# Another order for the same instructions: a written-out plan of a fused SSM-convolution and gated-MLP backward pass

## The chip, the cores and the metric

One core of a Trainium2 chip. The metric is the device time of one execution in microseconds (us), as a median of runs; a profile of one execution shows where it goes. The engines are TensorE (PE, matmuls; PEld is its weight load), VectorE (DVE), ScalarE (ACT), GpSimd (POOL) and SyncE (SP, which here issues every DMA).

## The reference, cut to what matters

The kernel computes a forward pass and all its gradients for a given `grad_out`, with S = 2048 tokens, D = 512, F = 1376, in bf16. The input x is normalised once and goes through two layers:

```python
xn = layernorm(x)
# layer A: shift convolution (4 taps), product with v, long convolution by FFT over 2S
k_shift = sum(k_pad[:, t:t + S, :] * shift_k[:, ks - 1 - t] for t in range(4))
kv = k_shift * v
y = irfft(rfft(kv) * rfft(ssm_k))[:S] + kv * ssm_D
# layer B: bilinear gated MLP
h = (xn @ w_gate) * (xn @ w_up)
out = x + xn * y + h @ w_down
```

The outputs are `out` and the gradients of x, k, v, of the shift taps, the long convolution's kernel and ssm_D, and of the three weight matrices (w_gate, w_up: D x F; w_down: F x D).

## The kernel before, in words

The kernel is written as a set of small steps, each on one engine, and an order for all of them. Helper objects stand in for the engines: a call such as `nc.vector.tensor_tensor` only records an `Op` (class `Eng`, line L173, which is why nearly every row of the profile carries L173). Consecutive matmuls into the same PSUM tile are joined to one PE step of up to 2200 columns. There are 2285 steps: 1009 of PE (3190 matmuls and transposes in all), 654 of DVE, 361 of ACT, 258 of SP (one DMA each) and 3 of POOL.

At the end `emit(PLAN)` decodes a string: a permutation of the 2285 steps, and then one bank number for each of 398 PSUM tiles (8 banks of 512 fp32 columns; a two-bank tile takes a neighbouring pair). It issues the steps in that order under a manual schedule. So each engine's queue holds its own steps in the order of the plan, and semaphores follow from what the steps read and write. A PSUM bank's next owner waits until the last reader of the owner before is through.

SP's DMAs go out in plan order from one queue, with eight semaphores taken in turn: a DMA waits for its own data and also for the landing of the eighth DMA before it, and all that stand behind it wait with it.

The steps by stage, with the names that matter below (n, r and j are indices that the code uses):

- Loads and layer norm: `xload`, `gtload` (columns of transposed grad_out, `goT`), the first MLP weights in two transfers (L364 and L368), `gload` (grad_out rows, `go`), `w_load(j)`. `ln` normalises x rows; `tr_rows` (L409 to L416) transposes them, on PE for rows under 8, by DMA transpose otherwise.
- `mlp_rows(j, r)` (L429 to L440): for six stages j of F, the gradient towards the hidden layer (`pd`, from goT, which needs only goT and weights) and the two gates (`pg`, from the normalised, transposed x). ACT, in some stages DVE, evicts; DVE forms the products. `hd_store` writes products to a DRAM buffer HD.
- `dw_gen(j)` (L589 to L606): weight gradients, groups of 16 matmuls accumulating over 16 row tiles. They lie among the other steps.
- `a_gen`: shift convolution and the first step of the Fourier transform for three signals (stored to AX). `s_gen` (`s_B`, `s_pw`, `s_Bi`): the middle step, products in the frequency domain, and the way back (stored to CX).
- `turn_gen` (L620 to L627): transposes of hidden products of stages 4 and 5, partly by DMA, partly on PE.
- The last part, for n = 0 to 7 (two of the 16 row tiles each): `c_load(n)` reads 1.5 MB of CX, `last_dft(n)` (24 matmuls) forms three signals, `c_dkv`, `c_y`, `c_o5` use them, `c_dsk` multiplies by k (`k_load`) and sums on PE with ones (8 matmuls per row tile). `hd_load(n)` (L645) reads HD by a DMA transpose into buffer n % 2, which must wait for the last matmul of n - 2 that reads it. `y_o(n, rr)` (11 matmuls, plus one with the identity for n = 7) and `y_x(n, rr)` (22) multiply its blocks by the three weight matrices for the output and for x's gradient; y_x has a chain of DVE steps behind it (L815 to L821, with ACT at L820) that ends the layer norm's gradient. `dk_pair` (seven DVE steps and a store) forms k's gradient. For n = 7 y_o(rr=1) runs in two halves of 256 columns.

Of the kernel before, what the change touches and what calls it, by code (L numbers as in the profile page):

```python
# [25 lines left out]
SB = [0, None, 1, 2, 3, 4]  # L26
# [12 lines left out]
def kernel(  # L39
# [895 lines left out]
    for n in range(NCH):  # L935
# [148 lines left out]
```

## Time and profile before

| what | value |
|---|---|
| time, median of 3 runs | 427.82 us (427.53 to 428.08) |
| the profiled execution | 426.92 us, of which the span of the core's instructions is 425.1 us |
| TensorE clock granted | 1.00 of full speed over the span |
| DMA | 127.27 MB, 299 GB/s on average, one queue at 94.4% of 16 engines' span |
| matmuls | first at 1.06 us, last ends at 420.10 us |
| largest group of PSUM evictions | ACT, 314 of them, 781 ns on average |

The span is the time from the first to the last instruction of the profiled execution; 1.8 us of the execution's time lie around it. A row of waits gives the engine and line, whom it waited for, the total in us, how often, and the longest. The chain of waits follows the work that ended last back to the start, each row with start, duration and what it was. Since all recorded steps have one line, tiles tell the steps apart: `PP` is PSUM, `big` the SBUF, `AX`, `CX`, `HD`, `KS` are DRAM buffers and `in_..._dram`, `out_dram` the inputs and outputs.

### The profile page before, as it was taken

The page shows a single profiled execution, that of the slowest core. Times are in us where ns is not written, and L with a number is a line of the kernel's source. Part 1 is how long each engine was busy: PE and PEld are TensorE (multiplying, and loading weights), DVE is VectorE, ACT ScalarE, POOL GpSimd, SP SyncE. Part 2 cuts the span into 40 slices and gives each one's busy share as a digit, 9 for nine tenths or more (in the row PEclk, how much of TensorE's full clock was granted, in tenths as well). Part 3 has the DMA queues.
Part 4 walks back from the last instruction along what each step waited for, and adds up shares of the span by engine and source line. Part 5 has one row for each costly group of instructions (what it writes and reads, how often), then busy time and mean ns, then how long its engine had stood idle before and what let it go on. Part 6 is the DMA issues. An engine that isn't in the chain of part 4 may idle for free.

```text
span 425.1 us, 8146 instructions
## 1 busy us (share of the span) xinstructions
PE 414.8 (98%) x3190; PEld 198.9 (47%) x3190; DVE 350.7 (82%) x684; ACT 257.8 (61%) x364; POOL 3.5 (1%) x9
## 2 busy tenths in 40 slices
PE   7999999999999999999999999999999999999995
PEld 4745555854554333544444334444444444444343
DVE  5999977998649989899999980325858898999996
ACT  4855988598644999888999953363414230422323
POOL 1000000000000000000000000000000000000000
PEclk9999999999999999999999999999999999999999
DMA  8999899999788879969889899999999999999953
GB/s 277 399 180 395 295 305 395 344 363 360 298 297 304 320 250 338 310 202 341 305 286 349 291 313 314 250 392 309 188 296 305 308 258 333 309 303 290 278 174 147
DMA packets 104222, 127.27 MB, mean 299 GB/s; under 512 B 63860, under 2 KB 73977, under 8 KB 103160
## 3 DMA queue, kind: packets, MB, share of 16 engines
q1 hardware_dynamic: 104184, 126.75, 94.4%
q8 instruction: 25, 0.41, 0.4%
q14 instruction: 13, 0.11, 0.1%
HBM read 57.10 MB, written 54.04 MB: 261 GB/s over the span
## 4 chain that ended last, share of the span: by engine, by line
PE 70%; DVE 14%; DMA 11%; issue 2%; ACT 2%; SPq 1%; ACTq 0%
PE PP L173 70%; DVE big L173 14%; DMA out_dram<-big 4%; DMA big<-CX 2%; DMA big<-in_k_dram 2%; ACT big L173 2%; SPq L173 1%; DMA big<-in_w_dram 1%; DMA big<-in_go_dram 1%; DMA big<-in_x_dram 1%; ACTq L1080 0%
## 5 line engine op out<-in xcount | busy, mean ns | idle before, releaser
L173 PE MATMUL PP<-big 128*128 128x512 bf16 (+7 forms) x3190 | 414.8, 351 | 5.3 <-DVE big L173 1.8
L173 DVE TENSOR_TENSOR big<-big 128x1024 bf16<-128x1024 bf16 (+2 forms) x465 | 268.1, 630 | 45.8 <-ACT big L173 36.7
L173 PEld LDWEIGHTS <-big 128*128 128x128 bf16 (+3 forms) x3190 | 198.9, 97 | 221.0 <-issue 64.4
L173 ACT CAST big<-PP 128x512 bf16<-128x512 f32 (+2 forms) x314 | 224.3, 781 | 87.1 <-PE PP L173 75.5
L173 ACT ACTIVATE big<-big 128x512 bf16<-128x512 f32 (+3 forms) x30 | 19.1, 642 | 50.1 <-DVE big L173 50.0
L173 DVE CAST big<-PP 128x512 bf16<-128x512 f32 (+1 forms) x37 | 32.4, 875 | 9.7 <-PE PP L173 5.1
L173 ACT COPY big<-PP 128x1024 bf16<-128x1024 bf16 x15 | 15.0, 1012 | 20.9 <-PE PP L173 20.8
L173 DVE SCALAR_TENSOR_TENSOR big<-big 128x1 f32<-128x1 f32 (+2 forms) x52 | 25.3, 499 | 0.3
L173 DVE SCALAR_TENSOR_TENSOR big<-big,PP 128x512 f32<-128x512 bf16 x14 | 9.6, 682 | 8.6 <-PE PP L173 8.6
L173 DVE BATCH_NORM_STATS2 big<-big 128x6 f32<-128x512 bf16 x16 | 10.5, 683 | 3.7 <-DMA big<-in_x_dram 3.7
L173 DVE TENSOR_TENSOR big<-big,PP 128x512 bf16<-128x512 bf16 x14 | 9.2, 681 | 1.1 <-PE PP L173 1.1
L173 DVE TENSOR_SCALAR big<-big 128x1 f32<-128x1 f32 (+1 forms) x28 | 6.8, 256 | 0.0
L173 POOL MEMSET big<- 128x1536 bf16 (+2 forms) x3 | 2.9, 950 | 252.3 <-PE PP L173 252.3
L173 ACT ACTIVATE big<-PP 128x512 f32<-128x512 f32 x2 | 1.2, 597 | 4.5 <-PE PP L173 4.5
L173 DVE BATCH_NORM_AGGREGATE big<-big 128x2 f32<-128x6 f32 x16 | 2.3, 169 | 0.1
L173 ACT ACT_TABLE_LOAD x1 | 1.3, 1283 | 0.7 <-PEq L1072 0.7
L173 DVE RECIPROCAL big<-big 128x2 f32<-128x2 f32 (+1 forms) x9 | 1.2, 151 | 0.6 <-ACT big L173 0.6
L173 DVE DVE_READ_ACCUMULATOR big<-big 128x1 f32 x16 | 1.3, 82 | 0.0
L173 DVE DVE_READ_ACCUMULATOR big<-big,PP 128x1 f32 x14 | 1.1, 81 | 0.0
L173 DVE MEMSET big<- 128x128 bf16 (+1 forms) x2 | 0.2, 112 | 0.8 <-PEq L1072 0.8
L173 DVE COPY big<-PP 128x1024 bf16<-128x1024 bf16 x1 | 0.7, 692 | 0.2 <-PE PP L173 0.2
L173 ACT ACTIVATION_READ_ACCUMULATOR big<-PP 128x1 f32 x2 | 0.4, 194 | 0.0
(6 smaller groups left out, 0.9 us busy)
## 6 DMA issues: line engine op xcount, KB each, us to landing
HD<-big SPq DMA_DIRECT2D x32, 384.0 KB, 5.8
AX<-big SPq DMA_DIRECT2D x16, 768.0 KB, 5.6
big<-AX SPq DMA_DIRECT2D x16, 768.0 KB, 5.5
CX<-big SPq DMA_DIRECT2D x16, 768.0 KB, 5.1
out_dram<-big SPq DMA_DIRECT2D x44, 256.0 KB, 3.5
big<-CX SPq DMA_DIRECT2D x7, 1536.0 KB, 8.3
big<-in_vK_dram SPq DMA_DIRECT2D x8, 512.0 KB, 5.3
big<-in_w_dram SPq DMA_DIRECT2D x4, 768.0 KB, 7.4
```

What stands on the lines that cost most here:

```text
L173: o.fns.append(lambda: f(*[fix(x) for x in a], **{kk: fix(x) for kk, x in k.items()}))
```

## The change

Only the string of the plan is another one:

```diff
-PLAN = "c-l=@V-TK6vu*dpcCx|7wr$(C?G1Kgd$Swcwr$(Cv$pS>e1C2|...
+PLAN = "c-l2r1N2`<(;m;pwrv}Y?W9S=CTVQjwr!(PV>fPW+eU4FzklEJojrH&-Pw8WJTqs{&I|y9fP#TTfM^g...
```

It decodes to the same 2285 steps, each once, in another order, and to other banks for 302 of the 398 PSUM tiles. Transfers over 500 KB keep their order among themselves. On PE 908 of 1009 steps stand at another place of PE's own queue (by 11.2 places on average, half of them by 4 or less, at most 110), on DVE 577 of 654 (3.8, at most 30), on ACT 276 of 361 (2.3, at most 29), on SP 206 of 258 (4.1, at most 56), on POOL none. Some of the places, decoded:

SP's first DMAs, before and after:

```text
before: x r2-3, x r6-7, goT 4-5, x r0, D row, weights 1st part, weights 2nd part,
        x r1, goT 3, x r4-5, goT 1, x r8-11, goT 0, goT 6-7, goT 2, ...
after:  x r1, x r0, x r2-3, x r6-7, goT 0, weights 1st part, goT 3, goT 1,
        goT 4-5, x r4-5, weights 2nd part, x r8-11, goT 6-7, D row, goT 2, ...
```

SP around hd_load(1), around c_load(4) and c_load(5), and ahead of c_load(7):

```text
before: dw_gen(j5) store, c_load 2, dkv_load 2 (two), c_dkv(n1) store, hd_load 1
after:  dw_gen(j5) store, c_load 2, hd_load 1, y_o(n0) store, c_dkv(n1) store, dkv_load 2

before: y_o(n1) store, hd_load 3, c_dkv(n1), c_load 4, y_load 3, dkv_load 4, ...
after:  hd_load 3, y_o(n1) store, c_load 4, dk_pair(0..) store, k_load for c_dsk(n3), ...

before: hd_load 4, turn_gen, c_load 5, k_load for c_dsk(n4), y_load 4, ...
after:  hd_load 4, y_load 4, k_load for c_dsk(n4), k_load for c_dsk(n5), ..., c_load 5

before: c_o5(n5) store, y_x(n4) store, dk_pair store, y_o(n5) store, c_load 7, ...
after:  y_x(n4) store, c_o5(n5) store, dk_pair store, c_load 7, ...
```

PE's last steps:

```text
before: y_x(7,0) and y_x(7,1) in turn with y_o(7,0) begun, c_dsk(7), rest of y_o(7,0),
        y_o(7,1) in two halves
after:  y_x(7,1), y_x(7,0), y_o(7,1) in two halves, c_dsk(7), y_o(7,0)
```

In the last part the matmuls of y_o and y_x of one row tile stand closer together than before, where those of several tiles alternate.

More of the change, by code (lines that the diff above doesn't have):

```diff
@@ new lines @@
+PLAN = "c-l2r1N2`<(;m;pwrv}Y?W9S=CTVQjwr!(PV>fPW+eU4FzklEJojrH&-Pw8WJTqs{&I|y9fP#TTfM^gMVn9rY1+gIx#D#c}7!pB2C<J*R8GHl?C7=|Pgwl`~%0PU`0;wPYB!rYu7>YnqC=2DFG9-af&<0XNQ)mb6As>{76p$YZKm}+E#h?RJgpSY|Izbnx2T5TLtb;Vr71Ba8_!L^eTv!huLmj9K^`QYYgyN75l0!PE0)yZa7z|aR5sZe(&>X5mHJAzmpax8Vfsh?)!Vnk=!=W*BgJZA{y2Dba1=C;zw1f=M1g66<7zv-ja##lYAwAT<aWDgB!WftZTcJ19#Mv+w#zRk70V|;rtb*0B1}4BZ=miU)2W*FVkQDpC4%i91U^lFVT38!DhrUn;>tZt80~?_qw1RKoTgVLyVLlv(1F#6bgYz&EzK7)a11yG%umNtvLHH6j!6DcThhYn3g}rbRPQX`?5i&t$NP#Ia71qNa;bXiEN8l%T0H@#%d;yc-S2zu4-~!};>u?EfKx#~bX)zt9#|(G{eu1As@hW7*Oqdz7U{-txU&A#Jd<2gn8$N-X@Dy%AcFcjR(eN4M#D5?c=Egi&9~)p^%!m2002ahTSQv|7QTz>J;$3(Sfd2wwPH+rZ49~(j_#OU&Pw-Q0jxDeyeumL7I&Q*y&<fY!8+ZYKLPPumMj>M^7=dFj2FAj_VJyCdM)(Rw<9J+)>u^1Oj*YQ3w!tRY6ko$gd<n7f9c;k1*bduc2keNOaS1fTxY!9NU_9)MUGP1O!znlsCt)1yigR%)PR7MJ8@u6toQB<TDbB&^xDl7&GMtICa31c%9@rCm;TDXKy|EA0hNG|*58y%k5)a`*T!ekGANI!qI1s<ULAV0vV+&f2+i)-r!J*iahG7CMfroJc4x*CSh(5wnSQ-b?U>ZV0=@=%&L|6tB<1iXdpU_cUg-5VHHKfMWfSOVh`jk3QSuBUm={T0h3Rn@hV@EoH?dT+ag_W=}R>9Lajiyr)Y)|L#44y^8QFH+>;w8L{SMVxU#o~Akuj388iMQ}J-od+g5AWjxe29<mF+Rbk_za(8HLQ*=@Fl*&*Z2nC;yau{GieshrqlEu=g=AYj6UGk_zjk&Z}B@UN9Cy%wV?`Bkt$JTI!iln7oNh_P=%V&_xJ<;h(F=aSe2?#b@~N=#ozFE`~&~QzwmGT2meJNBqAmuB_pRm(I`5_ppmp2Thl!nj-6;P?!?ZtifT|z%1imE3(cbe6q9089EwZvC_d$<1eB1@QE%!)wWv0&rk>P`&eH{&ONl5koyYF95_?bqDo9BvDJ7%il!8*yMcRXPs1OyVB2<)$QE{qEsVFrqpb@l)(okATN9k!Xm7olikup(V>PH__S6WE@p&NaG%#?+)QZ~v?IVdOPqLTCxm7>ygpK?<kDnsjNG>xSP^pMum7+OPXX$yT$<7g92pba#MzM#!CktWj~+DqeU7d@iOw43(PetJv?=m~A5skDuj(sJ5P-_Q@Vf{xG>+Cj_cApJ<+(Iq-YN9kMoOX|`0bd!$LArihtcjy`2rk^MSXXL~5Gbx{n1o<f~q36V$i8J%Bbb?;e3wlLa_&3VR**H62p+95>-iNDnod{OapLC7BqQB@a<=~v0i*s`x&dYD;9la*!O8lNG^INLIRk<2h=Rpj7gZ`9ZJcN;dC*vtRlm~MSuF17{IFH~zC>sAmf71+(&m%cH&*WGfgJW|{j>{kDANgD2@Km10V>usB=W$${$8#O7%k?-v7hqG@`ILZzj^;7^F@utRO$j*>CuY<MoP;OxBu>i7nDt*#P0lGeC8y%loQCIeT5e0}STvf(qWV0W8}KI_k4N!BUc@nV9(Ujv+K~%!VJ^Z&xfsXR;v7rkXgp2Noj8rg)#&;Qb>{h8f=lv8+=aVxH%_bRv^%HQ_?l1?YXVKKrMNUF(lXqGdvY&cz!@}?mgS6Ej>~fe?#)@WA}7<#+J|%Lmy}f-@-lA3jkzx`;iTG+n{ZRkqe(P{rqbM+Qd4UY&8z)+7BA*zoKN%X9A3@?xUjC^61tJA>8ISBTX0J*uA8`qe#Y6g6<616+M3(&O3tY{bQKrXVp>u^(vwt3OKTmit2ekmz2eurnoDU}Ew7ces+Q4mx|!?g7QV^1xGlHi_PmB`>TSNmcljRQ=Lh_dA8{?MtrfL`HqwInh9C12e#&pTl2*}HT0ooVXWCZR@=hwqjrAEf&`-3XzT@Zog5UE8{+hqxrur>^tl#nX`~xSGcG^ZeXeaHW-E=D_mlV=W`|79KTH9+!O)04)wfxBawV&?fpZI59$ARl>3mvROG>xQ{T|AI?^B(T3+xc@Is$I2*{=x&ar*_wLl3sGj4&F!`xTOx#(K=A~@>tCv8Kt@AkTKd@d+9#TBe^B7^wFt0PN(P$%_QSBr(~8al2vAEHW{WRWQDHh$$Wyp;^BId^GSXwDW~`}PtcV*LRV>N8L5XkNHiIxtMv<>rn9t+9O3CYTi57Z{Yd6$bcrD`C6>gNI8sX1>H(gw6Lq1k(|Ni;7wJ-6ub=A~KFjC$SDvK%Ij+Q$_>w>pN+L-t2YIn>(j>B3w`fxNjVJ4J-KR_RfG*SXyjM5qzjT2w@|S#w%St)<oww^@J*xZlDDTiqTvPtwoq9-*aRK>4YspsKrk8ms7m+XZh+g5^Qb&&SE<LCP<(OXOYg|;Wb0N8^e{yv>u7B}ME-c05gkIC@dP%Qn4f&hP%VjMtU+EdGC);?Bp4ZcQN-yX?{4ZCQlM1q1E67c)C>!;np3_@eSDH#Cd9GFDw%*Ye(opVdOQ|MjwW>6d27+>5KNXUD`aqk@BYmki^tL=ymS-yRR$u80eXVb_nS3Ix<f%T<cluth%P;zwsN9jqdQ(2=4f$BU(O<QRe67FfEx9N4#l+>V{H}j$Yw0Y1X&31#f9SXRgT9m><sWS<Kk85Vo&F?$Yg@@KV6UW|w2^=HXYD54<+-56upVMY_Cmhb_7bdv+!wZ=rKj|g-qJ_<ikn(=>nG_gmc_Jq7Td()T71iB{bhg*l!r1%GFSpjXq{xRJeD{X&0b4l>nM-piKMYa_D0fKQadKcC9OS>X);}A$S;z~PRLjCt0cF~meP`05=&tx<&>P3Gm_QLN-8U0&m@bTlbJG0ve|6OZaM6{T#z|(QSR7dyK9#ur=_++mfPmaJee;At*8~V!nQyb$|A{Sd8~vLx2ICl^4VqiR`S|+vQ560E0W)e*hf~%-pddvZDnn-ERm%$RF=yyDQDlvRk?4!$ue0X)vUZ#v@%w~p4e?0F56{<RJW0`Lw3q886~5ohOLwzq>|ON+O|q|%RAX4d!?3*k=3$B*2+5h(#A?<t73I*oK&^(GC}IvM42R$<%6`gHrCeKS$peX9qoawmq)fw`dUBhZv$+g)w7T7bJ-xBth05ot~Sm#N;m6nn`E<WktwoY4#-2RZw>4dYiI}MOF1NmWxO@A#@57|S~L69CRh*aX}zquy_N4}qD``?azu_wZ~H<9Sqp1vpV?p=Vnc11{cW$Tm2H*bHo_*`6uW0nZKRE|4>sDK*>js}(`>r^E;DSV&9cvJzAdnYw!yB+kM^xCvc)#r=GYQjYRl|}eP>_WH}=wgwlOx==GsQvWSeb^ePLT|n{Brpw$pamZrfvfZJsT+6}Hk=**;rsYizBpvm>_N-r4u|n;o@up58O~Pxg_!|8B4Cz4ftU_N%?MKkP3H9?heBDL-Lv><42PS2r*1Wjv$D@R+{ej$3j+V3|CYXZ9=}+v9j#kLU3{foJt>p51eJPOs>dys}sET>hse^rZfk<?*tf$jSe;nqJG3`9D_Jb9)j0#cF#UZ{k(`q@fr0f?m#3dm(S;O+B%f_mtks>v}!^*gx_5-oP7rBhTykJc+09qF%wPd3*2RsXV{8_7dLMJ9;PY>|MO8xAAE{-P?LMukNR8hR^g_UcgV=87t|-eYV%|Ilju%cz++@t9^~n^<m!KKlOQj){1#rU+j~-pO5qLKEX%$d~fdUe58-^!G6(3`vSjYOMSh6?i+lgPxMW`+1GkcALEm~hxhUpKGt7&Zy)Ge{4@W;7drSkYw3G^x%c%ce%N1nA7AF{{GjdgSAO0u`DMT2SN)nF@kM^rSNK+6;>UcOANSWj#1Hxj-|qK)sK52=zQ?EfJAdyV{A>TlANdWx>AQWUKlgKf$}iXxKka8cV;JOL`AOg5w|uAH_HX?=|K5M}AN(iZ<q!S5KlPveUw`Zu{H(w6IAOnEjI{7^L%a|_T((RhbMSD-?|OoeFkr|MzVr|%L<`wMqVStX4+s2Lzha3)((t<{3HSV&CkuZ#hwR~y|LqSvUHHedhF?5K$Qg2l+(AOxpus|(kS3%KF+$}~JJbm=!=GLyR1H_{nk5ghLjI69#18pFnUEor4h2HpP%nHO>W8ACS|}S@hk_wxXcO9o2BBOi5<Us#L%UEc6b~svp^!c_42?sF&@prhokN$<HB1eMY+9HeW`steNvIw^3Kc@jP%*R!HA1&gGu*V9VOA&{u3M^5D^v>2LeFr^hK6CGdl(*?hUQ^*=n+PQUSVt)7jD@2@L8A>CWHauFE0`1hEkz@=pTBAK4D~-9|nePVSCsSc7|PHcjy;}gn409*c6t8(P2!O7#4)hVM|yT4%?)#CoBv5!`{#;Ob+|P%5WmA3SWfP;Xqgu`i3cCZCD=Gg*)MHxEJn+2jOA(G%N}S!<XSvC>hp=$Kk7RGMoyh!<n!&Tn$gdpzt=l3!jH4VQ{z-o`q}SY&aJ#gjeBwcpk2Yi{W)x5jKRa;ZV2{UWAQdakv!Thd1FvxEU^oTj6E69S(;h;b=G(jt6oRMMY+C<w(=ukw#pc2w4b4IdZNkQr{zi5D7%hAmC>1Dv_F80L`La|F1yeh!7DuMpCZ}J3-WTB)La2D5yp58?nf5(IC<SMj;H0)I~v~wjDttIXz+;BNU8T5K)zZD1wa`g9t%Tl&I?~qDicdk(M&*BVy7p!dau17^y=jDsR(&Ph>=FK~x^6|H&e?f&E8I;J-EePvgH4Mb03i4N)`v4`l!8K@@@_$Veb0%5jwlxrj@`B2h8>&m%#O1dxCY|MOlgDh#Yqb|b+5@X8h?jbangGx|SAV3GR"
```

1 line of the change is left out of this document (removed).

## The prediction

> **What bounds the kernel now.** I read the page first, then busy time by stage, the waits, the chain of waits and the last microseconds. The page's list of engines:
>
> ```profile
> PE 414.8 (98%) x3190; PEld 198.9 (47%) x3190; DVE 350.7 (82%) x684; ACT 257.8 (61%) x364; POOL 3.5 (1%) x9
> ```
>
> PE is busy 98% of the span, but busy time includes overlap of pipelined matmuls, so I took start-to-start distances from the trace: 216 ns for a 128x512 matmul, 109 for 128x256, 82.5 for 128x192, 56 for 128x128, 42 for 128x96. Over 3190 matmuls they sum to 393.5 us. The first matmul starts at 1.06, the last ends at 420.10; the 25.6 us over the sum are mostly the small gaps of 0.12 to 0.14 at each group of narrow matmuls, which the new order keeps. Real stops of PE are few. Busy time by stage (columns: PE, PEld, DVE, ACT, POOL, each with its count; clock, DMA share, GB/s):
>
> ```profile
> 33.00:150.00 117.00, 116.88 (x943) 61.59 (x943) 98.47 (x165) 86.36 (x136) 0.00 (x0) 1.00 0.92 331
> 150.00:245.00 95.00, 95.00 (x958) 40.70 (x951) 91.89 (x167) 87.95 (x112) 0.00 (x0) 1.00 0.85 300
> 245.00:300.00 55.00, 55.00 (x376) 24.81 (x373) 23.05 (x42) 24.91 (x31) 1.47 (x2) 1.00 1.08 312
> 300.00:340.00 40.00, 39.22 (x269) 18.53 (x268) 31.30 (x70) 13.56 (x15) 0.00 (x0) 1.00 1.07 276
> 340.00:380.00 40.00, 39.27 (x210) 17.12 (x208) 37.89 (x78) 9.63 (x11) 0.00 (x0) 1.00 1.11 308
> ```
>
> From 33 to 300 PE alone sets the time (it never stops), although DVE and ACT are busy 97% and 93% of 150 to 245. From 340 on DVE is as full as PE. The waits that PE has (engine, who, total us, times, longest):
>
> ```profile
> PE PP L173 <- DVE big L173: 1.8, 2, 1.1
> PE PP L173 <- DMA big<-CX: 1.7, 2, 0.9
> ...
> PE PP L173 <- DMA big<-in_w_dram: 0.9, 1, 0.9
> ...
> PE PP L173 <- DMA big<-in_go_dram: 0.6, 1, 0.6
> ```
>
> In starts of matmuls these are 1.33 at 6.1 (first weights), 0.74 at 31.5 (go), then 0.97 at 335.6 and 1.10 at 394.5 (last_dft of n=4 and n=7 waits for c_load), 0.92 at 362.9 (DVE) and 0.45 at 380.0: 3.4 us late in the run. The chain of waits (start, us, what) shows the same places:
>
> ```profile
> 3.02 4.78 DMA big<-in_w_dram
> 7.84 5.84 PE PP L173 x48
> ...
> 28.56 4.52 DMA big<-in_go_dram
> 33.12 267.92 PE PP L173 x2270
> ...
> 350.23 7.92 DMA big<-in_k_dram
> 358.17 4.17 DVE big L173 x9
> ...
> 387.60 8.83 DMA big<-CX
> 396.46 23.65 PE PP L173 x143
> 420.51 0.72 ACTq L1080
> 421.25 0.42 DVE big L173
> ```
>
> From 301 to 387 it runs through DVE and its loads; at the end through c_load(n7), PE, ACT, DVE. After PE's end at 420.10 there are 5.0 us: the last y_x tail on DVE (421.25 to 421.68), its store (issued 421.86, landed 424.14) and 1.0 to the span's end at 425.1.
>
> The sum is made on the profiled run, 426.92 us, 0.90 below the median of 427.82; I add the 0.90 back at the end. For the new order I kept every instruction's duration from this trace, laid PE's matmuls end to end at the old pace, and asked of each what it waits for.
>
> **Start, +0.4 (-0.4 to +1.2).** SP now issues x0, x1 ahead, and the first weights have 1280 KB up to their end against 1409; queued transfers land at about 395 KB per us, so they land at about 7.4 instead of 7.80. PE begins with matmuls of mlp_rows(j0) at 7.4 where it had transposes at 6.1 and then a stop to 7.84: about even. The other half of the weights lands at about 12.2 (9.1 before); five groups of about 1 us each cover that, and without the cover it costs 3. DVE's 1.25 us wait for x1 at 8.2 goes. Against this, summing ACT's queue from 15 to 32 us, its evictions are due 1.0 to 1.2 us later than the old pace asks at 26 to 31, where old PE then lost 0.74 for go. What is left is 0.4. The move of w_load(j1) behind two DMA transposes has 3 us of slack.
>
> **Middle, 33 to 260, +0.7 (0 to +2.5).** The matmuls of weight gradients are shifted among MLP and transform work, up to 110 places, and banks differ for 302 of 398 slots. Summing ACT's and DVE's work queued before each matmul that needs it, the worst lateness is 0.2 in the old order, 0.25 to 0.40 in the new (around 150 and 220 to 241). A bank passes from one owner to the next 558 times. Time from the last matmul of one to the first of the next: the shortest past the start was 0.89, now 0.65, 0.67, 0.77 and 0.79. An eviction of 128x512 takes 0.60 and starts about 0.16 after its matmul; with the signal back 0.9 is needed. Four reuses fall short by 0.1 to 0.25 each, together 0.7. SP's moves here (the dw_gen(j3) store 9 places earlier, E tables later) delay no load that PE needs in time.
>
> **hd_load(n1), +0.3 (0 to +3.2).** The first y_o(1) matmul now comes at about 298.5, where n=1 began at 302.9, because PE's work before it is regrouped. This DMA transpose went out at 287.47 and landed at 300.31. It is now queued ahead of three small transfers, behind the dw_gen(j5) store, whose matmuls end 0.9 earlier; I put its issue at 286.3. The eight hd_loads took 9.4 to 12.8 from issue to landing. With 12.8 less the queue it no longer shares, it lands between 297 and 299; the unfavourable end is 301.8.
> [...]
>
> **Late part, 300 to 420, -2.0 (-3.4 to 0).** c_load(n4) follows hd_load(n3), which is now ahead of the y_o(n1) store and goes out at about 316 instead of 320.42: its landing moves from 336.94 to about 332.6 and is needed at 334.2, so 0.97 goes. c_load(n7) is now ahead of the y_o(n5) store: landing 393.4 for 396.42, needed at 394.5, and 1.10 goes. The k_load for c_dsk(n4) moves ahead of c_load(n5), so that DVE's wait of 2.04 at 356.1 (the chain's 7.92 row) goes, and most of its 2.00 at 318.8 for the y_x(n0) store. PE's 0.92 and 0.45 hang on DVE. hd_loads n2 to n7 are issued 1.0 to 4.5 earlier, and PE has 16.6 to 17.5 us of work between the buffer's last reader and next reader (14.9 to 17.5 before) against at most 12.8. Of 3.4 I take 2.0, as queues that move often open a smaller wait elsewhere.
>
> **Tail, -1.0 (-1.5 to 0).** Both y_x(n7) and the two halves of y_o(n7,rr1) now come before c_dsk(n7) and y_o(n7,rr0). After PE's end only an eviction of 0.60 and a 128 KB store (1.7) remain: 3.3 us with the 1.0 at the end, against 5.0. But DVE must have finished its last dk_pair and y_x too. Each DVE end is bounded by a PE time plus the DVE work queued behind it: the worst was 403.66 + 17.64 at y_x(n6,rr1), now 401.94 + 18.78, 0.6 earlier at PE's old pace; summing ACT and DVE together gives 1.4. DVE, not PE, is then last; 1.0 is between.
>
> Sum: 0.4 + 0.7 + 0.3 - 2.0 - 1.0 = -1.6, so 425.3 in a profiled run, 426.2 as a median.
>
> **Rivals.** (a) Slower: banks come free too late. Reuses within 1.5 us between 33 and 245 rise from 30 to 80. If evictions queued behind others make each of the 50 added ones 0.08 us late on average, PE loses 4.0 there instead of 0.7: 429.5. It decides from 0.05 each, when 2.5 cancels the gain. For it: DVE's 97% and ACT's 93%. Against: the 37 old reuses within 1.5 cost PE nothing visible.
> [...]
> (b) Slower: hd_load(n1) lands at 301.8, PE stops 3.2 instead of 0.3: 429.1. For it: its 12.84 before; against: fewer transfers around it.
> (c) No change: DVE stays as late as it was and the 3.4 us after it too, so late and tail gains shrink to what start and middle cost, 1.4: 427.8. For it: DVE's near-full rows after 340.
> (d) Slower: ACT's queue at the start, due 1.2 late already, holds PE for 3 instead of 0.4: 428.8. For it: PE must wait for every eviction there; against: go4 to go7 cost old PE 0.74 at the same place, which this covers.
> (e) Faster still: all 3.4 us of late stops vanish, the tail gives 1.4 and the front costs nothing beyond 0.4: 423.4.
>
> **Chances.** Forecast 0.40 (425.0 to 426.9), (e) 0.17, (c) 0.13, (a) 0.15, (b) 0.09, (d) 0.06. About 0.2%, 0.86 us, is what a measurement of this kernel can tell from no change; so faster 0.57, same 0.13, slower 0.30. The range reaches to (e) and past (a): 423.6 to 430.0; the forecast's own is 425.0 to 426.9.
>
> **What would show it.** Right: no PE wait for CX at n=4 and n=7, no DVE wait for in_k near 356, PE's end near 419.5, the last DVE work near 420.1, under 4 us between PE's end and the span's. Wrong: PE waits for ACT or DVE between 33 and 245 summing to over 2 us (a); a PE wait for HD near 298 (b); the last DVE work at 421.7 or later (c); PE at the go wait of 31.5 later than before by over 2 (d).

## The result, and the profile after

| what | before | after |
|---|---|---|
| time, median of 13 runs each on one chip | 427.85 us (425.90 to 430.18) | 432.77 us (427.31 to 435.19) |
| ratio, 95% interval | | 1.0076 (1.0047 to 1.0105) |
| the profiled execution / its span | 426.92 / 425.1 us | 432.90 / 431.1 us |
| last matmul ends / from there to the span's end | 420.10 / 5.0 us | 425.03 / 6.1 us |

The new order is slower, by about 1%, where 426.2 us was forecast. The ratios here and below leave out runs that lie over 1.5% above the fastest of their kernel, here three of the new one's, so this ratio is smaller than that of the medians (1.0115).

The page of the profile after, its span, engines and granted clock (tenths of full speed in 40 slices):

```profile
span 431.1 us, 8080 instructions
PE 411.8 (96%) x3134; PEld 199.5 (46%) x3190; DVE 353.1 (82%) x684; ACT 256.5 (60%) x364; POOL 3.5 (1%) x9
PEclk9999999999999999999999999999999899999998
```

PE's share fell from 98% to 96%, though its work is the same. (56 matmul records are missing from this trace, so the counts of matmuls below are a little low.) The 32nd slice, 334 to 345 us, has a lower clock. The stages, as shown of before (columns: stretch, its length, PE, PEld, DVE, ACT, POOL, clock, DMA share, GB/s):

```profile
33.00:150.00 117.00, 115.80 (x908) 61.74 (x929) 99.62 (x167) 84.97 (x136) 0.00 (x0) 1.00 0.90 325
150.00:245.00 95.00, 92.54 (x951) 39.53 (x954) 92.35 (x169) 87.79 (x113) 0.00 (x0) 1.00 0.89 310
245.00:300.00 55.00, 53.36 (x339) 24.57 (x344) 23.51 (x40) 22.52 (x30) 1.47 (x2) 1.00 1.04 304
300.00:340.00 40.00, 37.60 (x254) 17.49 (x260) 31.27 (x70) 13.25 (x15) 0.00 (x0) 1.00 1.09 286
340.00:380.00 40.00, 39.63 (x234) 17.93 (x232) 37.21 (x76) 10.62 (x12) 0.00 (x0) 0.96 1.02 278
```

PE's busy time is now short of the stretch in every row. Up to 245 that is for the most part the missing records: in experiment 4, which has the same order there and all its records, the first two rows read 116.52 and 94.64. PE loses most between 300 and 340, and the clock row of 340 to 380 stands at 0.96 where it was 1.00. What PE waited for (total us, times, longest; gaps without a known releaser are left out):

```profile
PE PP L173 <- DMA big<-CX: 2.3, 2, 2.0
PE PP L173 <- DMA big<-big: 1.7, 2, 0.9
PE PP L173 <- DMA big<-in_w_dram: 1.5, 1, 1.5
PE PP L173 <- ACT big L173: 1.2, 1, 1.2
PE PP L173 <- DVE big L173: 1.1, 1, 1.1
PE PP L173 <- DMA big<-AX: 0.3, 1, 0.3
```

The go wait of before is gone and DVE's second wait too. New are a wait for ACT and two for DMA transposes (0.86 at 27.0 and 0.80 at 410.4), and the CX wait is 2.0 at its longest where it was 0.9. The chain of waits (start, us, what):

```profile
156.54 1.86 PE PP L173 x21
158.39 8.52 DMA big<-AX
...
246.03 7.17 DMA CX<-big
254.35 3.47 PE PP L173 x42
...
331.33 8.20 DMA big<-CX
339.57 5.18 PE PP L173 x39
...
416.74 4.31 DMA out_dram<-big
421.07 5.89 DVE big L173 x13
```

The transfers shown stand at places where PE or DVE lost time: a load of AX, a *store* to CX at 246, c_load(n4) at 331, and a store of k's gradient at 417, behind which DVE ends.

To put sizes on the places I took PE's lateness: for the same amount of matmul work done (nominal durations of the prediction), how much later a kernel starts it than the profiled before. In the profile after it is 1.2 us at 33, 2.25 at 245, 3.4 at 255, 3.2 at 330, 6.2 at 345, 4.9 at the end (the missing records leave about 0.2 open).

**The stop near 254.** PE's rows there:

```profile
249.71 3.43 PE L173 MATMUL PP<-big 128*128 128x512 bf16 x27
254.35 1.82 PE L173 MATMUL PP<-big 32*64 32x512 bf16 x21 [1.21 <-ACT big L173]
```

PE waits for ACT at s_Bi(i7,pr2); but ACT itself waits to overwrite a buffer until CX store #1586 has read it (issued 246.03, landed 253.19: the chain's 7.17; in before 243.91 to 249.43). In the new order a 384 KB piece of c_load(n0), #1753, stands on SP ahead of the two CX stores.

**The stop near 339, and the store ahead of it.** SP's own rows around it, of before and then of after:

```profile
312.45 0.49 SPq L173 DMA_DIRECT2D out_dram<-big  x1
...
320.42 8.18 SPq L173 DMA_TRANSPOSE big<-HD  x1
...
329.95 0.53 SPq L173 DMA_DIRECT2D big<-CX  x1
```

```profile
319.01 0.33 SPq L173 DMA_DIRECT2D out_dram<-big  x1
...
320.89 9.72 SPq L173 DMA_TRANSPOSE big<-HD  x1
...
331.33 0.38 SPq L173 DMA_DIRECT2D big<-CX  x1
```

The first row of each is the store of y_x(n0). It went out at 312.45, now at 319.01: on DVE the last steps of y_x(n0,rr1) (L819, #1840, and #1842) now stand behind the first ones of y_x(n1,rr0), which wait for PE until 312.5. SP stands still from 314.5 until the store may go, and hd_load(n3) (row two, which then holds SP for 9.72) and c_load(n4) (row three) are queued behind it. c_load(n4) lands at 339.53, PE wanted it at 337.6. Then the clock (stretch, PE busy, clock, DMA share, GB/s):

```profile
338.00:340.00 2.00, 0.43 (x8) 1.00 1.03 392
340.00:342.00 2.00, 2.00 (x21) 0.55 1.53 263
342.00:344.00 2.00, 2.00 (x7) 0.59 0.87 222
344.00:346.00 2.00, 1.95 (x16) 1.00 1.09 364
```

After a stop of 1.98 us the granted clock is at 0.50 from 340.21 to 343.62, 3.41 us, which costs 1.7 us more: (0.45 + 0.41) x 2.

### The profile page after: what moved, and what is told of

Its sections match the earlier page's. It is cut to its first block, busy times and chain, and to the rows that moved or that the text cites. A ratio compares the mean times of both kernels' runs of the same rounds, so it can differ in the third digit from the quotient of the medians.

```text
span 431.1 us, 8080 instructions
## 1 busy us (share of the span) xinstructions
PE 411.8 (96%) x3134; PEld 199.5 (46%) x3190; DVE 353.1 (82%) x684; ACT 256.5 (60%) x364; POOL 3.5 (1%) x9
## 4 chain that ended last, share of the span: by engine, by line
PE 67%; DVE 14%; DMA 10%; ACT 4%; issue 3%; SPq 1%; DVEq 0%; ACTq 0%
PE PP L173 67%; DVE big L173 14%; ACT big L173 4%; DMA out_dram<-big 3%; DMA big<-AX 2%; DMA big<-CX 2%; DMA CX<-big 2%; DMA big<-in_k_dram 1%; DMA big<-in_w_dram 1%; SPq L173 1%; DVEq L1080 0%; DVEq L173 0%; ACTq L173 0%
## 5 line engine op out<-in xcount | busy, mean ns | idle before, releaser
L173 PE MATMUL PP<-big 128*128 128x512 bf16 (+8 forms) x3134 | 411.8, 351 | 13.3 <-issue 2.7
L173 DVE TENSOR_TENSOR big<-big 128x1024 bf16<-128x1024 bf16 (+5 forms) x465 | 268.9, 629 | 46.1 <-ACT big L173 31.9
L173 ACT CAST big<-PP 128x1024 bf16<-128x1024 f32 (+3 forms) x314 | 222.9, 783 | 115.3 <-PE PP L173 79.7
```

Of the source, the lines that this page charges most:

```text
L173: o.fns.append(lambda: f(*[fix(x) for x in a], **{kk: fix(x) for kk, x in k.items()}))
```

## The experiments

**Theory A**: the loss is three places, each a transfer that small moves on SP and DVE made late: the start, the CX store, c_load(n4), with half clock behind the longer stops. **Rivals**: banks that come free too late (rival (a) of the prediction), the DMA queue being full whatever the order, the seams and scatter. Every ratio is to before on the same chip. Steps are named by their number in the plan. The banks went with the order in each part.

**1. Old order up to 271 us, new behind it.**

```diff
-steps 1 to 1690 in the new order
+steps 1 to 1690 in the order of before
```

> The old order for its first 1690 steps (up to about 271 us), the new order for the rest. Theory A (a few late transfers: PE's lateness against the old kernel is 1.2 us at 33, 3.4 at 260, 6.0 at 345, 4.9 at its end): the front's 3.4 us vanish, c_load(n4) still comes late, since what delays it lies behind 300 us: 3 to 3.5 us below the new kernel, 1 to 3 above the old one. Theory B (banks come free too late everywhere): the late part keeps its tight banks, few of which are tight, so nearly the old time. Theory C (late part alone is at fault): no change against the new kernel.

Measured: 427.33 us, ratio 0.9999 (0.9977 to 1.0020), lower than A expected. PE was 1.0 late from 33 to 260, then stopped 2.2 at c_load(n4), was 4.1 late at 345 and 1.2 at its end. So the new order's late part alone costs nothing on balance: its stop and its gains cancel. The loss needs the first 271 us.

**2. New order up to 281 us, old behind it.**

```diff
-steps 1741 to 2285 in the new order
+steps 1741 to 2285 in the order of before
```

> The new order for its first 1740 steps (up to about 281 us), the old order for the rest. Theory A: PE is 3.4 us late at 281 us; behind it the old late part with its four stops: old time + 2.5 to 3.5 us. Theory B: the same or more, as all tight banks are kept. Theory C: the old time.

Measured: 431.01 us, ratio 1.0066 (1.0039 to 1.0093). PE is 2.7 late at 60, 3.4 at 245, 4.8 at 255 (a stop of 1.4 at s_Bi(i7,pr2)) and 5.8 at the end. The front alone brings nearly the whole loss.

**3. The store of y_x(n0) early again.**

```diff
 DVE:
+y_x(n0,rr1) #1840, y_x(n0,rr0) #1815
 y_x(n1,rr0) #1875, #1878, #1876
+y_x(n0,rr1) #1842, c_dkv(n2) #1848
 y_x(n1,rr0) #1877, #1879
-#1840, #1815, c_dsk, #1848, c_y, c_dsk, #1842
+c_dsk, c_y, c_dsk
 ACT: #1841 right behind #1840
```

> The new order, with the five steps that hold the y_x(n0) store moved before y_x(n1)'s DVE steps: DVE L819 and L821 of y_x(n0), ACT L820 between them, and DVE's dv product of c_dkv(n2). SP then stands behind that store until about 314.5 instead of 319.0, so hd_load(n3) goes out when its buffer is free (318.7 instead of 320.9) and c_load(n4) lands near 337 instead of 339.5. Theory A: PE's stop of 2 us at last_dft(n4) and the half clock for 3.4 us behind it (1.7 us lost) vanish: 2.5 to 3.7 us below the new kernel. Rival (the DMA engines are simply full there, whatever SP's order): c_load(n4) still lands at 339 and the time stays.

Measured: 431.54 us, ratio 1.0065 (1.0039 to 1.0091): less gained than expected. In its profile (433.38 us, 1.8 over the median) the store goes out at 316.66 and the stop at last_dft(n4) is gone (lateness falls by 0.5 from 330 to 345, where it grew by 3.1), but the stop at the CX store was 2.35 us this time with half clock behind it (lateness 1.5 at 250, 5.5 at 255). c_load(n4) landed at 339.49, no earlier than in the profile after (339.53); the stop is gone because PE came to it 2.1 us later. With PE's lateness taken off on both sides the landing is 2.1 us earlier, as the mechanism asks. One repair does not show in the time while the other stop can grow.

**4. Ten more 128x512 matmuls ahead of last_dft(n4)** (2.2 us of extra work, whose result nobody reads).

```diff
+if n == 4:
+    for i in range(10):
+        MM(py[1][:, 0, :], lhsT=ones1[:], rhs=<ones, 512 columns>, start=True, stop=True)
 for sig in (1, 0, 2): ...
```

> The new order, with 10 more 128x512 matmuls (2.2 us of PE, on the tile of ones, into last_dft(n4)'s own PSUM tile, which last_dft overwrites) ahead of last_dft(n4). They fill PE's stop for c_load(n4) and change nothing that is computed. If the stop is what halves the granted clock from 340 to 343.7 us: clock 1.00 there, 1.7 us below the new kernel, PE's lateness behind it smaller by that much. If the half clock has another cause: clock as before, time the same or up to 0.2 longer.

Measured: 429.45 us, ratio 1.0016 (0.9993 to 1.0039), so more work gives less time than the new kernel's 1.0076. The clock, in the same stretches:

```profile
338.00:340.00 2.00, 2.00 (x28) 1.00 1.51 176
340.00:342.00 2.00, 2.00 (x17) 1.00 0.81 207
342.00:344.00 2.00, 2.00 (x11) 1.00 1.07 373
```

2.2 us of work cover a stop of 2 us and take away the 1.7 of half clock. This profiled execution took 426.11 us, 3.3 under the median, with all other parts of the new order in it.

**5. The c_load(n0) piece back behind the CX stores.**

```diff
 SP: k_load(n0)
-c_load(n0) #1753, CX stores #1585, #1586
+CX stores #1585, #1586, c_load(n0) #1753
```

> The new order with one DMA moved: the third quarter of c_load(n0) (384 KB) goes out behind the two CX stores of s_Bi(i6) instead of ahead of them, as in the old order. Theory A: in the four profiles so far with the new front, PE lost 1.3, 1.5, 4.1 and 0.0 us at s_Bi(i7) near 253 us, since ACT could not evict into the CX buffer until the second of these stores had landed (7.2 us after issue; 5.5 in the old order); with 384 KB less ahead it lands about 1.3 us earlier and that stop shrinks to 0 to 0.5: 1.2 to 1.7 us below the new kernel. Rival (ACT's own queue or the banks cause the stop): time unchanged, stop still there though the store has landed.

Measured: 430.44 us, ratio 1.0082 (1.0047 to 1.0116) to a before of 427.43. The stop near 254 is gone (lateness 4.78 at 250, 4.87 at 255), but this profile was 3.95 late at 60 already and stopped 2.2 at c_load(n4). Half clock followed this stop, and also a stop of 1.93 at 5.8 for the first weights; no other profile has half clock at its start. The time alone is inconclusive.

**6. Both repairs (3 and 5).**

```diff
+both diffs above
```

> The new order with that DMA behind the CX stores and, as before, the steps that hold the y_x(n0) store moved ahead of y_x(n1)'s DVE steps. Theory A: no stop at 253 and none at last_dft(n4), no half clock behind either: 428 to 429.5, so 3.5 to 4.5 us below the new kernel; what stays against the forecast of 426.2 is the start (0.7 us from 8 to 33 us) and the end. Rival (more such narrow places that change from run to run): above 430.

Measured: 428.16 us, ratio 1.0030 (0.9999 to 1.0061). PE is 1.2 late at 245, 1.05 at 255, 1.4 at 345, 0.03 at its end; its longest wait for CX:

```profile
PE PP L173 <- DMA big<-CX: 1.2, 2, 0.8
```

The two repairs take 0.46 of the 0.76%. What is left, 1.3 us, is of the start's size.

**7. Experiment 1 with the early store.**

```diff
+diff of 3 on the kernel of 1
```

> The old order up to about 271 us, then the new one with the y_x(n0) store early. With the new back alone PE lost 3.1 us at last_dft(n4) (2.2 of waiting, the rest half clock) and gained 2.7 us behind it. Theory A: without the stop about 424.5, 3 us below the old kernel and faster than both. Rival (the DMA engines are full there): c_load(n4) as late as before, 427.3.

Measured: 426.27 us, ratio 0.9964 (0.9938 to 0.9990), faster than both kernels, though by less than the 3 us expected. It was run again with the last group:

> The kernel with the order of before to 271 us, the new order behind it and the store of y_x(n0) early, a second time and beside the three above: its ratio was 0.9964 with an interval of 0.9938 to 0.9990. Theory A (it is faster by the late part's gains of about 1.5 us): 0.9940 to 0.9990. Rival B (the first time was luck of the draw): 0.999 to 1.002.

Measured: 426.18 us, ratio 0.9992 (0.9972 to 1.0012). The two intervals share 0.9972 to 0.9990, so a gain of about 1 us is likely and no more is shown. The stop at last_dft(n4) is still 2.1 and 2.2 us in the two profiles; half clock followed in the second only. So the early store did not take this stop away here.

**8. The same, with dk_pair's last steps on DVE behind work that does not need its buffer.**

```diff
 DVE, at the end:
-dk_pair(r014) #2256, y_x(n7,rr1) #2274, dk_pair #2258, y_x(n7,rr0) #2250, #2252
+y_x(n7,rr1) #2274, y_x(n7,rr0) #2250, #2252, dk_pair(r014) #2256, #2258
```

> As the one before, and at the end dk_pair(12)'s last two DVE steps 2 places earlier, and dk_pair(14)'s first write to the shared buffer, which waits for dk_pair(12)'s store, behind three DVE steps of y_x(n7) that need not wait. DVE stood 2.1 us there in the new kernel's profile (store landing 4.3 us after issue, 2.0 in the old one). Theory: 0.5 to 1.5 us less than the kernel before it, 423 to 424. Rival (PE's end sets the span's end): no change.

Measured: 426.12 us, ratio 0.9973 (0.9947 to 1.0000). DVE's wait for the dk store is down to 0.2 us and the tail is 4.5 us after PE's end instead of 5.3, but the time does not tell it from experiment 7. The stop at last_dft(n4) is 2.17 us here, with half clock behind it.

**9. Meant as the best: 8, and last_dft(n4) 1.5 us later in PE's order, with two small transfers moved on SP.**

```diff
 PE:
-last_dft(n4), y_o(n3,rr1) fb4, y_o(n3,rr1) fb8
+y_o(n3,rr1) fb4, y_o(n3,rr1) fb8, last_dft(n4)
 SP:
-y_o(n1) store #1894, c_load(n4)
+c_load(n4), y_o(n1) store #1894
-dk_pair store #2180, turn_gen #1726
+turn_gen #1726, dk_pair store #2180
```

> Meant to beat both: the order of before to 271 us, then the new order with the store of y_x(n0) early, last_dft(n4) 1.5 us later in PE's order (behind the rest of y_o(n3,rr1)), c_load(n4) ahead of one y_o store on SP, the last turn_gen transpose ahead of a dk store, and dk_pair's last steps on DVE behind work that does not need its buffer. Theory A (stops that wait for a landing, with the half clock behind them, are what is left): the stop at last_dft(n4) falls from 2.1 to under 0.7, the clock stays at 1.000 there, the tail is about 4.5: 424.5 (423.5 to 425.5), ratio 0.990 to 0.996. Rival B (the DMA queue is full, so a load moved ahead only makes another late by as much): the stop comes back at a later load, 426.2 within 0.6, ratio 0.996 to 0.998.

Measured: 427.33 us, ratio 1.0012 (0.9990 to 1.0034): a miss. The stop at last_dft(n4) is gone, but PE waits 0.30 at 337.0 for ACT's eviction of c_dkv(n4), 1.01 at 342.8 for DVE's y_o(n3,rr1) and 0.42 at 351.5 for hd_load(n4), so lateness rises from -1.1 at 336 to 1.2 at 363. Delaying last_dft(n4) delays its readers: here its rival held.

**10. The new order for the start only.** First to 85 us, then to 60 us.

```diff
-steps 671 to 2285 (second kernel: 405 to 2285) in the new order
+these in the order of before
```

> The new order and banks for the first 670 steps (to about 85 us), the order and banks of before for all that follows. Theory A (the start of the new order costs PE about 1 us by 33 us and about 0.6 more by 60 us, apart from anything later): PE is 1.0 to 1.9 us later than in before at 85 us and stays so, the time is about 428.8 (428.2 to 429.5), ratio 1.002 to 1.005. Rival B (what the profiles show at the start is scatter of the first loads, and the cost of the new order lies in the later stops alone): 427.5 within 0.5, ratio 0.999 to 1.001.

> The new order and banks for the first 404 steps only (to about 60 us), the order and banks of before for the rest. In the profiles so far the kernels with the new start are 1.6 us later than before at 60 us in the mean (0.6 to 4.0), those with the old one 0.1 earlier. Theory A (the start's cost is made before 60 us, at the transposes of x and the first generator steps): 429.0 (428.3 to 430.3), ratio 1.002 to 1.007, PE 1 to 3 us late at 60 us and no later after. Rival B (what the kernel with the new start to 85 us lost, 3.7 us, was made at its seam near 100 us and after): 427.4 within 0.6, ratio 0.999 to 1.001.

Measured: 430.52 us, ratio 1.0086 (1.0058 to 1.0114), and 431.29 us, ratio 1.0091 (1.0061 to 1.0121), six runs each: both more than expected. The first is 0.8 late at 60 and loses 1.4 at 101.8 to a DVE eviction behind its seam; the second is 1.1 late at 60 and 3.4 at 80, with a stop of 0.95 for a load of v. So in these profiles the seams add 1.4 to 2.3 us to the start's 0.8 and 1.1. Both profiled executions lie well under their medians, by 2.5 and 2.35 us; where the others lost that is not shown, and these two kernels do not isolate the start.

**11. The old order for the first 60 us, the new for the rest; and the same with both repairs.**

```diff
-steps 1 to 415 in the new order
+steps 1 to 415 in the order of before      (second kernel: and the diffs of 3 and 5)
```

> The order and banks of before for the first 415 steps (to about 60 us), the new ones for the rest, nothing repaired. Theory A (start +1.9, CX stop near 253 us +1 to +2, late part about 0 with its stop at last_dft(n4)): the new kernel less the start, 428.7 (427.8 to 430.0), ratio 1.001 to 1.006; the stop at s_Bi(i7,pr2) is there in about the size it had (1.2 us or more). Rival B (the CX stop is made by the lateness and the queue that the new start leaves): no stop there, 427.3, ratio 0.998 to 1.001.

> The same with the old first 60 us, and both repairs: the c_load(n0) piece behind the two CX stores, and the store of y_x(n0) early. Theory A (start, CX stop and the late store are the whole cost): 426.3 (425.5 to 427.2), as the kernel with the old order to 271 us and the early store (ratio 0.9964), so ratio 0.994 to 0.999. Rival B (the new order costs something more between 60 and 271 us, at banks or evictions): 427.5 to 428.5.

Measured: 431.24 us, ratio 1.0114 (1.0076 to 1.0152), and 427.78 us, ratio 1.0017 (0.9999 to 1.0035). The seam costs here too: lateness from 60 to 80 goes from 0.3 to 1.3 and from -0.3 to 2.0. The first misses its forecast; but it shows the CX stop without the new start (PE waits for ACT, as in the new kernel):

```profile
253.79 2.47 PE L173 MATMUL PP<-big 32*64 32x512 bf16 x24 [0.94 <-ACT big L173]
```

and the repairs take 3.5 us off it, 431.24 to 427.78. The second misses its forecast of 426.3 too and lies where its rival has it, at something more that is lost between 60 and 271 us: the seam, and 0.7 that both lose from 80 to 245.

**12. Before, with one instruction moved: #1753 ahead of the CX stores.**

```diff
 SP: k_load(n0)
+c_load(n0) #1753
 CX stores #1585, #1586
-c_load(n0) #1753
```

> The kernel before with one instruction moved: the c_load(n0) piece #1753 stands on SP ahead of the two CX stores #1585 and #1586, as in the new order. Theory A (that one move makes the stop near 253 us): PE stops 1.0 to 2.5 us at s_Bi(i7,pr2) near 252, the stores land about 7 us after issue instead of 5.5, and the time is about 428.8 (428.0 to 430.0), since part of the lateness is taken up by the wait for c_load(n4) near 336, and more where half clock follows the stop. Rival B (the stop needs the lateness and the queue of the new order as well): no stop over 0.3 us there, 427.5 within 0.5.

Measured: 427.02 us, ratio 0.9999 (0.9980 to 1.0019): the rival. Store #1586 does land late in its profile (issued 244.04, landed 251.17: 7.1 us, against 5.5), and ACT waits for it; but in PE's old order PE is only 0.4 late from it. The stop needs the late store *and* the new order around it.

**13. Before, with only DVE's steps moved as in the new order.**

```diff
 DVE:
-y_x(n0,rr1) #1840
 c_dkv(n2), c_dsk, dk_pair
-y_x(n0,rr1) #1842, y_x(n0,rr0) #1815
 y_x(n1,rr0) #1875, #1876, c_y(n2), y_x(n1,rr0) #1877, c_dsk
+y_x(n0,rr1) #1840, y_x(n0,rr0) #1815, y_x(n0,rr1) #1842
 ACT: #1841 three steps later
```

> The kernel before with only this moved: on DVE the last steps of y_x(n0,rr1) (#1840, #1842) and of y_x(n0,rr0) (#1815) stand behind the first steps of y_x(n1,rr0), with ACT's step between them; SP's order is that of before. Theory A (the late store of y_x(n0) holds SP, and so hd_load(n3) and c_load(n4)): the store issues near 318 instead of 312.5, hd_load(n3) near 320 instead of 317, c_load(n4) lands near 339 instead of 336.9, the stop at last_dft(n4) grows from 0.8 to 2.5 to 3.5 us, and half clock follows in part of the executions: 430.0 (429.0 to 431.5). Rival B (c_load(n4) is late in the new order for the whole set of moved small transfers, and the store alone moves it by less than 1 us): 427.5 to 428.3.

Measured: 428.93 us, ratio 1.0045 (1.0025 to 1.0065), just under the range expected. SP's order is untouched; its rows, PE's and the clock's:

```profile
316.94 0.34 SPq L173 DMA_DIRECT2D out_dram<-big  x1
...
320.52 10.67 SPq L173 DMA_TRANSPOSE big<-HD  x1
...
331.92 0.53 SPq L173 DMA_DIRECT2D big<-CX  x1
```

```profile
339.15 4.16 PE L173 MATMUL PP<-big 128*32 128x512 bf16 x30 [3.61 <-DMA big<-CX]
```

```profile
340.00:342.00 2.00, 2.00 (x16) 0.62 1.03 392
342.00:344.00 2.00, 2.00 (x7) 0.52 1.06 406
```

c_load(n4) goes out 2.0 later than in before and lands at 339.10 instead of 336.94. PE, 1.2 us early in this execution, asks for it 0.7 sooner, so the stop grows from 0.78 to 3.61, and half clock follows. hd_load(n3) goes out at the same time as in before (320.42 there; the expectation's 317 is a misreading); but the small transfers now go out just ahead of it, and it holds SP for 10.67 instead of 8.18. PE is 5.0 us later at 345 than at 330 and gets 2.0 back by its end. Three DVE steps a few places later, with an ACT step, cost 1.9 us of time.

## Why the prediction was wrong

The profiled span grew by 6.0 us. Point by point, forecast against the profile after, and the mean over all profiles that hold the part in its new form:

| term | forecast | profile after | mean over profiles |
|---|---|---|---|
| start, to 60 us | +0.4 | +1.2 | +1.7 (8 profiles against 9 with the old start) |
| middle, 60 to 245 | +0.7 | +1.0 | +0.7 (6) |
| CX store, 250 to 255 | none | +1.3 | +1.6 (5) |
| hd_load(n1), 255 to 330 | +0.3 | -0.2 | -0.1 (12) |
| c_load(n4), 330 to 345 | -1.0 | +3.1 | +3.2 (4, without the early store or extra work) |
| rest of the late part | -1.0 | -1.3 | -1.5 (10, without extra work or experiment 9) |
| tail | -1.0 | +1.1 | +0.3 (10) |

The column after adds up to the 6.0 with -0.1 between 245 and 250; the late part's -2.0 is split by its terms, 0.97 for c_load(n4).

**The step that failed most: the landing of c_load(n4).** It was forecast to go out behind an hd_load(n3) issued at 316, to land at 332.6 and to be needed at 334.2. hd_load(n3) went out at 320.89, c_load(n4) landed at 339.53, and PE wanted it at 337.6. PE is 3.2 late by then; with that taken off, the need was right and the landing 3.7 too late. It has two parts.

The first is what holds hd_load(n3). I took it to be the y_o(n1) store, which it overtakes in the new order. In before that store went out at 317.32, and what SP waited for until 320.42 was the landing of c_load(n3), the eighth DMA ahead of it. It is the longest wait in this row of SP's waits from 300 on:

```profile
SPq L173 <- DMA big<-CX: 8.2, 3, 2.8
```

c_load(n3) is the eighth ahead in the new order too. It went out and landed earlier there, at 319.55, or 316.4 without PE's lateness, so the 316 was nearly met, but by luck and not by the overtaking. Then the y_x(n0) store, which I had not followed to the DVE steps that had moved behind a wait for PE, held hd_load(n3) until 320.89. This and the 0.4 make 1.7 of the 3.7.

The second is the time from there to the landing of c_load(n4). I kept the 16.5 us of before; it took 18.6. Experiment 13 shows that a late y_x(n0) store can make the whole stop in the old order, there too with 18.6. But the store is not all of it in the new order. Without the late store the stop falls to 0 to 0.8 in the three profiles with the new front (3, 6, the second of 11), where that time is 17.2 to 18.0, and stays at 2.06 to 2.23 in the three with the old front (7 twice, 8), where it is 19.0 to 19.3. So the rival of a full queue holds in part, and what makes that time differ was not settled. Experiment 1 has the late part and the tail alone in the new order: -3.0 was forecast for them, and the time did not change.

**The CX stores.** Of SP's moves up to 260 I asked only whether they delay a *load* that PE needs. That a store's *landing* holds an eviction buffer, and so PE, was not in the sum at all. With #1753 back behind the stores (experiments 5, 6 and the second kernel of 11) the place costs 0.2 in the mean, with it ahead 1.6 (0.2 to 4.3 in five profiles).

**The half clock** was not in the sum either: 1.7 us each time that it followed a stop (1.72 in the profile after), on top of the stop.

**The start** was mis-sized: right in sign, +1.7 instead of +0.4 (+1.4 without experiment 5, where half clock followed the wait for the first weights). At 8 us new and old starts are even (0.1 and 0.3 in the mean), as forecast, so the weights' terms held. The loss comes after. About 0.5 goes in small steps between 12 and 24, where no wait shows. Then PE waits at mlp_rows(j0,r10) for a DMA transpose of x, which landed at 27.77 in the profile after:

```profile
27.82 6.35 PE L173 MATMUL PP<-big 128*128 128x512 bf16 x39 [0.86 <-DMA big<-big]
```

This takes the place of the go wait (0.58 in before), and about 0.5 more is lost from 33 to 60 in the mean (nothing in this profile). ACT's queue, which I weighed for 26 to 31, is not what PE waits for there; the transpose is. How the small losses arise was not settled, nor was the start isolated without a seam.

**The tail** went the wrong way: the forecast bounded DVE's end by PE and by DVE's own queue, and left out that dk_pair waits for the store of the dk_pair before (issued at 416.74, 4.31 to its landing):

```profile
421.07 0.69 DVE L173 TENSOR_TENSOR big<-big 128x1024 bf16<-128x1024 bf16 x1 [2.08 <-DMA out_dram<-big]
```

In the ten profiles with this order of the tail it follows that landing: 3.9 us after PE's end where the store took 2.0 and 2.2 us (4, and 7 again), which is the gain forecast, and 6.0 to 6.3 where it took 3.9 to 4.5.

**What held.** No stop at hd_load(n1), save one of 0.69 in one later profile; the other late stops mostly gone (PE stops 0.28 at c_load(n7), 0.92 in before; none at 363, 0.73 in before), though one of 0.80 for a DMA transpose is new at 410.4. DVE's k_load wait near 356 is gone, but one of 2.9 stands at 338 instead. With the old front and the early store these gains seem to reach the time, by about 1 us. The middle's 0.7 was met in size by luck as far as is known: most of it is lost between 156 and 204, not around 150 or from 220 to 241 where the prediction had its engines latest, and no wait for ACT or DVE shows there.

**The rivals.** (a) fell: between 33 and 245 PE has no wait on ACT or DVE in its list, only 0.3 for AX and twelve issue gaps of 0.2 at most, which stand only in traces with missing matmul records. 302 other banks cost no wait there that the profile after shows. (b) fell: hd_load(n1) took 289.19 to 300.62, 11.4 us for 1.77 MB, or 155 GB/s, where it took 12.84 in before. (c) and (d) fell in their mechanism; (d) had the right place and sign. Three readings in the prediction are off without weight here: the go wait given at 31.5 stands at 32.54 to 33.12, the tight reuses of before are 30 in one sentence and 37 in another, and the range's lower end, 423.6, does not reach (e)'s 423.4.

## What to carry to other kernels

When instructions of one DMA queue are reordered, follow each large transfer back through *every* small one that stands ahead of it to the engine step that releases it, and to the landing that its own turn waits for (here that of the eighth DMA ahead). In experiment 13 three late DVE steps delayed a load that goes out 15 us after the store they hold. Give a store that frees a buffer the same care as a load: its landing is somebody's start (the one at 253.19 in the profile after, behind which ACT's eviction and PE at 254.35 go on). Read the granted clock behind a stop of TensorE (here a stop of 1.98 us cost 1.7 more by the clock that followed it), and judge a hybrid of two orders by its profile, since the seam has a price of its own.

## What the runs showed of the hardware that I had not expected

**Half clock after stops near 2 us.** In the profiles, stops of 1.93, 1.98, 2.17 to 2.35 (six of them) and 3.61 us were each followed by a stretch at a clock of 0.5, 3.41 us long in the profile after; one of 2.06 (experiment 7) and all of 1.81 or less were not. One such phase takes the mean clock of a run to an estimated 0.996, as 1.7 us are lost of 425. A stretch at half clock also follows PE's last matmul (from 424.73 in before and 428.95 in the profile after, 4.6 and 3.9 us behind it), where it costs nothing; profiles without another had a mean of 0.997 or more. At 0.996 or less stood all 11 runs of experiment 13, whose profile has the 3.61 stop, 9 of 13 of the new kernel, 4 of 12 with the extra matmuls, and 9 of the 117 runs of before beside the experiments. The new kernel's nine have a mean of 433.3 us, its other four 429.2. What sets the clock is not shown; of these stops, the shortest with half clock behind it is 1.93 us and the longest without it 2.06.

**The last of a transfer's landing records can come late.** In the profile after, the store of dk_pair that DVE waits for in the tail has 16 landing records: 15 stand by 418.74, the last at 421.05, and DVE went on at 421.07. Of the 162 transfers of that execution whose 16 records can be told apart, 18 have the last one over 1 us behind the 15th. The same store took 2.0 to 4.5 us in the ten profiles with this order of the tail, so here a margin of 1 us on its landing was no margin.
